# First batch's x turned as whole fp32 numbers, one head at a time, and split on the way out of PSUM

## The chip, the cores and the metric

The kernel runs on one core of one Trainium2 chip. The metric is the device time of one execution in microseconds (us). TensorE (PE) multiplies matrices, VectorE (DVE), ScalarE (ACT) and GpSimd (POOL) work elementwise, and SyncE (SP) issues every DMA of this kernel, in one order.

## The reference

For each of 8 batches and 8 heads, 512 tokens of x read 32 states, and the 32 states read the tokens:

```python
B, H, S, Ns, D = (8, 8, 512, 32, 64)
scores = scale * np.matmul(x, state.transpose(0, 1, 3, 2))      # then a softmax over the states
xread = np.matmul(a, state)
scores2 = scale * np.matmul(state, x.transpose(0, 1, 3, 2))     # then a softmax over the tokens
sread = np.matmul(a2, x)
return np.concatenate([xread, sread], axis=2)
```

The result, seen as 544 rows of 512 numbers for each batch, goes through a mixture of 4 single-head causal attention experts (head size 64, the two best experts of each row, weighted by a softmax of their gate logits):

```python
logits = x @ w_gate
topk = np.argpartition(-logits, K, axis=-1)[..., :K]            # K = 2
q = x @ wq[e]; k = x @ wk[e]; v = x @ wv[e]
scores = np.where(causal, -1000000000.0, scale * (q @ k.transpose(0, 2, 1)))
ye = a @ v @ wo[e]
out += mask[..., None] * w[:, :, kk:kk + 1] * ye
```

Inputs and output are fp32, the output has 8 x 544 x 512 numbers.

## The kernel before

**One list of steps.** The program first records every instruction as a step (class `Steps`), and `st.run(ORDER)` then issues them all from one line of a loop, which is why nearly every row of the profile names L265. `ORDER` holds three stored tables: the order of all steps, the engine that takes a step which two engines can do, and the buffer that each step gets. So the order on every engine, SP's DMAs among them, is the one that the tables say, and a changed table moves instructions anywhere in the program.

**Numbers in two parts.** A product in TensorE takes fp16 operands, so a fp32 number is kept as a high fp16 part (ACT writes it) and a low one (DVE's SCALAR_TENSOR_TENSOR, or two POOL instructions, subtract the high part), made by `hi_lo`. Three products of parts stand for one product.

**A batch.** `load(b)` fetches x in two halves of 256 tokens (tile `xn`, 512 KB each, two buffers) and the states (`sn`). `front(b)` makes the block matrix `bd` of the states, splits x into `xh` (`parts_of_x`), turns it into `xT`, multiplies `xT` with `bd` to the scores, makes their softmax (`eb`, then `at`), and from these and the split weights `wn` the keys `kt`, the values `v` and the queries `qf`, which are split into `qh` and turned by a DMA transpose into `qm`. Its last part, `side(b)`, does the same for the states (`state_scores`, `e2`, `a`, a DMA transpose into `a2t`, a product `a2t,xh`). `probs(b)` is the expert attention (scores `kt,qm`, probabilities `p`, split `ph`, DMA transpose `pt`), `reads(b)` multiplies `v,pt`, weighs the result (`z`, `zh`, DMA transpose) and multiplies with `wo`; every second batch `tail` treats the 2 x 32 state rows.

**The first batch** is made another way. Its `xh` is turned by TensorE, as 16-bit numbers (32 transposes `identh,xh`, 128 x 128 each), and copied out of PSUM into `xT` by ACT or DVE; `bd0` and `xT` give the scores of one 128-token tile and two heads at a time; the products `gs`, `at` behind the softmax are fp32. The weights are loaded behind both halves of the first x (`marks["l"]`):

```python
wfs, wg_ = load_weights(marks["l"])
```

Ahead of it TensorE gets matmuls on a tile of zeros (the `FILL` list: 35 of them, `bank<-zeros` in the profile), whose result nobody reads.

Of the kernel before, what the change touches and what calls it, by code (L numbers as in the profile page):

```python
# [18 lines left out]
CFG = dict(FILL=(1.0, 1.4, 1.8, 2.2, 2.6, 3.0, 3.4, 3.8, 4.2, 4.6, 5.0, 8.0, 8.5, 9.0, 9.5, 10.0, 10.5, 11.0, 11.5, 13.6, 14.0, 14.4, 14.8, 15.2, 15.6, 16.0, 16.4, 17.0, 17.4, 17.8, 18.2, 18.6, 19.0, 41.0, 41.2), RA=-1, RG=1, RV=2, RK=2, ZL=3, GP=1, PT=4, ZM=4, SM=4, QM=4, SIDE=32, FB=1, PX=1, PA=2, LB=1, xn=2, W0=-33, PACE=37.0, LAG=2,  # L19
# [9 lines left out]
        "!%AF+6QCvrLV4T*MQJ%agjKi!CPENxh1IwmgQ)`6!WCE%>tiw62F<V>Rl?fX3b#XJObQKf4YtPS*aR!%T1*BZR0o@48;ry)a2+<p;#8iVL0z"
        "nZ>#-%)!_riN8es`)i%;M=l%yBX2{&MSd<oy69lnAt7@0fcBZ$JK=rxp~H_!ne!&~T%PvJYfgR;~Ie?Uj<iCwV=Zp8P%*bn>SPl&*uVH5s>F"  # L30
        "Yp_N;AZ>^192!0!frSgKfoUl{0qY{B3C5E!Pp-SC*p8){0JkkDviW&Sc$e^6B>Y@U>t^GO&W!OlW;Un$1vQAV{j@W#^M?@4QC?Z3=H6Z5SyD"
        ")be@ORXck7oxI7;h;B1V_ad<q&;{cq1+i?yyqv{k7BTG~akF_W{Zo}rZ5ToH-+<}WQKE~k5*ny^CbgWJBIR-|c1h^RMPzp?lEoccw#$Ff`>r"
        "zT=NfB@-cBIbKiDF@8szO~T6?Ub1v<rLV8mdo`DI!LsM7SG!&{}Fht!NK+qjj_wThmG0hYcwTwW0kOlMmo}YD5PyF-E~tm>M@wV~UN3@H9rH"
# [235 lines left out]
def state_read_then_moe_attention(ctx: ExitStack, tc: tile.TileContext, x, state, w_gate, wq, wk, wv, wo, out):  # L269
# [220 lines left out]
    def load(b, after=None):  # L490
# [561 lines left out]
```

## Time and profile before

| | us |
|---|---|
| median of 3 runs | 307.17 |
| the three runs | 307.17, 305.06, 308.19 |
| the profiled execution | 310.0 |
| its span in the trace | 308.2 |

The profiled execution is a run of its own, 2.8 us above the median; 1.8 us of it lie outside the span. Busy times and stamps below are counted in us from the start of the span. The mean granted TensorE clock of the span is 0.983 of full speed (2.4 GHz; the lower of its two levels, 1.2 GHz, reads as 0.5).

### The profile page before, as it was taken

What the parts mean: (1) busy time and instruction counts of PE and PEld (TensorE: products, weight loads), DVE (VectorE), ACT (ScalarE), POOL (GpSimd) and SP (SyncE); (2) the same over time, 40 slices, a digit from 0 to 9 for tenths busy, and PEclk for the clock granted to TensorE, in tenths of its full rate; (3) what the DMA queues carried; (4) which work ended last, traced back from release to release, by engine and by line L of the source; (5) the groups of instructions that cost most, each with busy time, mean ns of one, the idle gap of its engine ahead of it and who ended that gap; (6) DMA issues with size and microseconds to landing.
All of it is one profiled execution on the core that took longest, in us unless ns stands there. A gap on an engine that the chain in (4) does not pass through costs nothing.

```text
span 308.2 us, 8993 instructions
## 1 busy us (share of the span) xinstructions
PE 285.8 (93%) x3323; PEld 193.7 (63%) x3323; DVE 260.0 (84%) x745; ACT 226.1 (73%) x690; POOL 151.9 (49%) x222
## 2 busy tenths in 40 slices
PE   8988799978999997999989799989999899999995
PEld 3555486655664756567764579747667668666763
DVE  3899799896899968799979979999997987878653
ACT  4678698886988967688977797879859955536532
POOL 7132454747663754549846874356366313511200
PEclk9999989997999997999999999999999999999999
DMA  8969689999799999889999999698368497398974
GB/s 194 223 124 203 154 156 183 234 177 172 138 202 203 168 180 213 171 177 197 207 142 245 185 234 175 125 185 178 83 146 176 91 209 126 95 172 205 184 213 152
DMA packets 165260, 53.95 MB, mean 175 GB/s; under 512 B 144096, under 2 KB 160736, under 8 KB 165216
## 3 DMA queue, kind: packets, MB, share of 16 engines
q1 hardware_dynamic: 165216, 53.37, 89.2%
q8 instruction: 26, 0.43, 0.6%
q14 instruction: 18, 0.15, 0.2%
HBM read 11.02 MB, written 8.91 MB: 65 GB/s over the span
## 4 chain that ended last, share of the span: by engine, by line
PE 46%; DVE 21%; DMA 14%; ACT 12%; issue 4%; POOL 3%; SPq 0%; DVEq 0%; ACTq 0%; POOLq 0%
PE bank L265 46%; DMA xn<-in_x_dram 4%; DMA qm<-qh 4%; DVE mx L265 3%; DMA a2t<-a 3%; ACT p L265 2%; ACT z L265 2%; DMA pt<-ph 2%; DVE xh L265 2%; DVE mb L265 2%; DMA z<-zh 1%; DVE eb L265 1%; DVE qf L265 1%; DVE sbm L265 1%; DVE z L265 1%
## 5 line engine op out<-in xcount | busy, mean ns | idle before, releaser
L265 PE MATMUL bank<-kt,qm 128*128 128x128 f16 (+7 forms) x384 | 48.4, 305 | 4.6 <-DMA qm<-qh 4.0
L265 PE MATMUL bank<-gs,at 128*128 128x260 f16 (+3 forms) x368 | 50.7, 284 | 1.1 <-DVE eb L265 0.7
L265 PE MATMUL bank<-wo_n,z 128*128 128x512 f16 (+1 forms) x198 | 46.5, 373 | 2.8 <-DMA z<-zh 2.3
L265 PE MATMUL bank<-v,pt 128*128 128x192 f16 x480 | 45.5, 251 | 2.7 <-DVE kt L265 1.5
L265 PEld LDWEIGHTS <-pt 128*128 128x128 f16 x480 | 41.0, 100 | 6.7 <-issue 4.0
L265 PEld LDWEIGHTS <-at 128*128 128x128 f16 x336 | 32.1, 98 | 8.5 <-issue 2.3
L265 ACT ACTIVATE p<-bank,mx 128x128 f32<-128x128 f32 (+3 forms) x64 | 33.3, 526 | 4.3 <-DVE mx L265 3.9
L265 PEld LDWEIGHTS <-qm 128*128 128x128 f16 (+1 forms) x384 | 23.5, 98 | 18.7 <-DMA qm<-qh 4.6
L265 DVE TENSOR_REDUCE mx<-bank 128x1 f32<-128x128 f32 (+3 forms) x64 | 28.8, 478 | 7.7 <-PE bank L265 7.3
L265 POOL TENSOR_TENSOR ph<-p,ph 128x768 f16<-128x768 f32 (+1 forms) x15 | 28.1, 1875 | 7.4 <-ACT ph L265 4.8
L265 PEld LDWEIGHTS <-z 128*128 128x128 f16 x198 | 18.1, 98 | 21.7 <-DMA z<-zh 3.8
L265 ACT ACTIVATE o<-bank 128x512 f32<-128x512 f32 x30 | 17.8, 596 | 11.9 <-PE bank L265 11.8
L265 ACT ACTIVATE z<-bank,c 128x64 f32<-128x64 f32 x87 | 20.4, 320 | 6.8 <-PE bank L265 6.1
L265 ACT ACTIVATE xh<-xn 128x512 f16<-128x512 f32 x32 | 19.1, 629 | 7.3 <-DMA xn<-in_x_dram 6.4
L265 PE MATMUL bank<-at,gs 128*128 128x512 f16 (+1 forms) x92 | 24.2, 399 | 0.3 <-DVE m L265 0.3
L265 DVE SCALAR_TENSOR_TENSOR xh<-xn,xh 128x512 f16<-128x512 f32 x27 | 19.5, 741 | 3.9 <-ACT xh L265 3.8
L265 POOL TENSOR_TENSOR qh<-qf,qh 128x768 f16<-128x768 f32 x11 | 18.4, 1680 | 5.0 <-ACT qh L265 4.9
L265 POOL TENSOR_TENSOR eb<-eb,sbm 128x512 f32<-128x512 f32 x11 | 12.4, 1130 | 13.4 <-DVE sbm L265 12.0
L265 POOL TENSOR_TENSOR z<-z 128x128 f32<-128x128 f32 x15 | 7.0, 468 | 21.7 <-DVE z L265 9.5
L265 ACT ACTIVATE ph<-p 128x768 f16<-128x768 f32 (+1 forms) x17 | 15.6, 918 | 2.1 <-DMA pt<-ph 2.1
L265 ACT ACTIVATE gs<-bank 128x512 f16<-128x512 f32 (+2 forms) x29 | 13.7, 496 | 4.7 <-PE bank L265 4.6
L265 PEld LDWEIGHTS <-xh 128*128 128x128 f16 x416 | 15.1, 101 | 2.1 <-issue 0.8
(213 smaller groups left out, 663.9 us busy)
## 6 DMA issues: line engine op xcount, KB each, us to landing
out_dram<-o SPq DMA_DIRECT2D x33, 256.0 KB, 2.8
xn<-in_x_dram SPq DMA_DIRECT2D x16, 512.0 KB, 4.8
sn<-in_state_dram SPq DMA_DIRECT2D x8, 64.0 KB, 4.2
p<-in_moe_wo_dram SPq DMA_DIRECT2D x2, 256.0 KB, 4.0
z<-zh SPq DMA_TRANSPOSE x29, 2.8
xT<-xh SPq DMA_TRANSPOSE x28, 3.3
p<-in_moe_wq_dram SPq DMA_DIRECT2D x1, 384.0 KB, 5.3
p<-in_moe_wv_dram SPq DMA_DIRECT2D x1, 384.0 KB, 4.8
```

The costliest lines, as they stand in the source:

```text
L265: f(**{k: v.ap() if isinstance(v, View) else v for k, v in kw.items()})
```

## The change

**The first batch's x.** TensorE now turns `xn` itself: 16 fp32 transposes of 128 x 128, each one head of 256 tokens (two tokens beside each other in a partition). Four of them fill a PSUM bank; ACT writes the high part out of it into `xT`, DVE the low part. `xT` is seen as [P, 2, 2, H, P] for it. The states of batch 0 are loaded twice beside each other (`sn2`, two DMAs of 64 KB), turned by two transposes, and written into `bd2`; the scores come as 24 products of 64 columns for each half of x. `xh` of batch 0 is still needed by the product `a2t,xh`, and its 4 pairs of splits now stand behind `marks["A"]`, which is behind the softmax. `state_scores` of batch 0 has 48 products of 256 columns in place of 24 of 512, with two maxima and two sums to be joined.

**Around it.** `xn` has four buffers in place of two; the weights are fetched in the order wv, wk, wq, and behind the first half of x alone; `tmt` has one buffer in place of two; 11 of the 35 zero matmuls have another due time; and all three tables of `ORDER` are new.

What it does to SP's queue at the start of the program (`xn` is x, `sn` the states, `p` the staged weights). Before:

```order
L265 DMA xn_88<-in_x_dram 128x8x128
L265 DMA xn_89<-in_x_dram 128x8x128
L265 DMA sn_87<-in_state_dram 128x2x64 x2
L265 DMA p_0_112<-in_moe_wq_dram 128x12x64
L265 DMA p_1_113<-in_moe_wk_dram 128x4x64
L265 DMA wg_111<-in_moe_w_gate_dram 128x4x4
L265 DMA p_2_114<-in_moe_wv_dram 128x4x64
L265 DMA p_2_114<-in_moe_wv_dram 128x12x64
L265 DMA p_1_113<-in_moe_wk_dram 128x12x64
L265 DMA p_0_112<-in_moe_wq_dram 128x4x64
L265 DMA xn_88<-in_x_dram 128x8x128
```

and now:

```order
L265 DMA xn_89<-in_x_dram 128x8x128
L265 DMA sn_0_88<-in_state_dram 128x2x64 x2
L265 DMA xn_90<-in_x_dram 128x8x128
L265 DMA xn_91<-in_x_dram 128x8x128
L265 DMA sn_87<-in_state_dram 128x2x64
L265 DMA p_0_115<-in_moe_wv_dram 128x12x64
L265 DMA wg_114<-in_moe_w_gate_dram 128x4x4
L265 DMA p_0_115<-in_moe_wv_dram 128x4x64
L265 DMA xn_92<-in_x_dram 128x8x128
L265 DMA p_1_116<-in_moe_wk_dram 128x12x64
L265 DMA p_2_117<-in_moe_wq_dram 128x4x64
L265 DMA p_2_117<-in_moe_wq_dram 128x12x64
```

The two state loads stand ahead of the second half of x, and both halves of batch 1's x (`xn_91`, `xn_92`) ahead of the weights wk and wq.

DVE's first work on data, before:

```order
L265 SCALAR_TENSOR_TENSOR xh_92<-xn_88,xh_92 128x512 x2
L265 SCALAR_TENSOR_TENSOR xh_93<-xn_89,xh_93 128x512 x2
L265 COPY xT_96<-bank_79 128x512
L265 SCALAR_TENSOR_TENSOR bd_0_90<-bank_82,bd_0_90 64x4x32 x2
L265 COPY xT_96<-bank_84 128x512 x2
L265 TENSOR_REDUCE mb_116<-bank_80 128x16
```

and now:

```order
L265 SCALAR_TENSOR_TENSOR xT_99<-bank_82,xT_99 128x512
L265 SCALAR_TENSOR_TENSOR xT_99<-bank_83,xT_99 128x512
L265 SCALAR_TENSOR_TENSOR bd_0_93<-bank_86,bd_0_93 64x256 x2
L265 SCALAR_TENSOR_TENSOR xT_99<-bank_80,xT_99 128x512
L265 SCALAR_TENSOR_TENSOR xT_99<-bank_81,xT_99 128x512
L265 TENSOR_REDUCE mb_119<-bank_84 128x16
```

Three copies are gone from the stretch ahead of the scores, and four low parts of `xh` stand behind the softmax now (three of them on DVE).

SP's queue where the queries of batch 1 are turned (`qm`), before:

```order
L265 DMA_TRANSPOSE pt_0_155<-ph_153 128x12x128
L265 DMA_TRANSPOSE pt_0_168<-ph_154 128x12x128
L265 DMA_TRANSPOSE xT_96<-xh_94 128x8x128
L265 DMA xn_89<-in_x_dram 128x8x128
L265 DMA_TRANSPOSE qm_134<-qh_142 128x12x128
```

and now:

```order
L265 DMA xn_90<-in_x_dram 128x8x128
L265 DMA xn_89<-in_x_dram 128x8x128
L265 DMA_TRANSPOSE pt_0_160<-ph_158 128x12x128
L265 DMA_TRANSPOSE pt_0_173<-ph_159 128x12x128
L265 DMA_TRANSPOSE xT_99<-xh_95 128x8x128 x2
L265 DMA_TRANSPOSE qm_137<-qh_145 128x12x128
```

The load of x that stood directly ahead of the first `qm` is ahead of both `pt` transposes now, and a second `xT` transpose stands in its place.

The diff, without the stored tables:

```diff
-CFG = dict(FILL=(1.0, 1.4, 1.8, 2.2, 2.6, 3.0, 3.4, 3.8, 4.2, 4.6, 5.0, 8.0, 8.5, 9.0, 9.5, 10.0, 10.5, 11.0, 11.5, 13.6, 14.0, 14.4, 14.8, 15.2, 15.6, 16.0, 16.4, 17.0, 17.4, 17.8, 18.2, 18.6, 19.0, 41.0, 41.2), RA=-1, RG=1, RV=2, RK=2, ZL=3, GP=1, PT=4, ZM=4, SM=4, QM=4, SIDE=32, FB=1, PX=1, PA=2, LB=1, xn=2, W0=-33, PACE=37.0, LAG=2,
+CFG = dict(FILL=(1.0, 1.4, 1.8, 2.2, 2.6, 3.0, 3.4, 3.8, 4.2, 4.6, 5.0, 8.0, 8.5, 9.0, 9.5, 10.0, 10.5, 11.0, 11.5, 13.6, 14.0, 14.4, 41.0, 41.2, 7.0, 7.0, 7.0, 7.0, 7.0, 7.0, 7.0, 7.0, 7.0, 7.0, 7.0), RA=-1, RG=1, RV=2, RK=2, ZL=3, GP=1, PT=4, ZM=4, SM=4, QM=4, SIDE=32, FB=1, PX=1, PA=2, LB=1, xn=4, W0=-33, PACE=37.0, LAG=2,
            FRONT=1.5, FSPAN=1.0, TSPAN=1.3, TOFF=1.2, KT=3, p32=3, ph=2, at=1, et=1, gs=1, xh=4, a2=1, o=4, sn=1, qf=2,
...
         st.dma(wg_, w_gate.rearrange("(k p) e -> p k e", p=P), 0.2, after=after)
-        for w in (wq, wk, wv):
+        for w in (wv, wk, wq):
...
             sns[b // 2] = st.buf("sn", [P, 2, 2, D], F32, bufs=CFG["sn"])
-            load_state(b, after)
+            if b == 0:
+                twice["sn"] = st.buf("sn2", [P, 2, 2, D])
+                for r in range(2):
+                    st.dma(twice["sn"][:, :, r], state[0].rearrange("(j c) n d -> n j c d", c=2), 0.4)
+            else:
+                load_state(b, after)
             if b > 0:
...
             xns[b].append(xn)
+            if u == 0:
+                marks["h"] = marks["l"]
         if b == 0:
...
-        bd = st.buf("bd0", [P, 2, H // 2, 2 * NS], F16) if whole else st.buf("bd", [P, 2, P], F16, bufs=2)
...
-        if whole:
-            fill(bd, 0.0)
-        tp = bank("tp")
-        st.transposes([(tp[:, :P], sn[:, b % 2].rearrange("p c d -> p (c d)"))], ident, 0.11, into=[bd])
...
-        turned = tp[:, :P].rearrange("p (n j) -> p j n", n=NS)
+        tp = bank("tp")
         if whole:
+            sn = twice["sn"]
+            bd = st.buf("bd2", [P, 2, 2, 2 * P], F16)
+            fill(bd, 0.0)
+            st.transposes([(tp[:, c * P:(c + 1) * P], sn[:, c].rearrange("p r d -> p (r d)")) for c in range(2)], ident, 0.22, into=[bd])
+            for r in range(2):
+                hi_lo(2 * P, bd[HC[r], 0, r], bd[HC[r], 1, r], tp[HC[r], :2 * P], 128.0)
+            bd32 = st.buf("bd32", [P, P], bufs=CFG["FB"])
             for c in range(2):
-                hi_lo(P, bd[HC[c], 0, :, c * NS:(c + 1) * NS], bd[HC[c], 1, :, c * NS:(c + 1) * NS], turned[HC[c]], 128.0)
+                act(P, by_head(bd32[HC[c]]), tp[HC[c], c * P:(c + 1) * P].rearrange("p (n j) -> p j n", n=NS), scale=128.0)
         else:
+            bd = st.buf("bd", [P, 2, P], F16, bufs=2)
+            st.transposes([(tp[:, :P], sn[:, b % 2].rearrange("p c d -> p (c d)"))], ident, 0.11, into=[bd])
+            turned = tp[:, :P].rearrange("p (n j) -> p j n", n=NS)
             hi_lo(P, by_head(bd[:, 0]), by_head(bd[:, 1]), turned, 128.0)
-        if whole:
-            bd32 = st.buf("bd32", [P, P], bufs=CFG["FB"])
-            act(P, by_head(bd32), turned, scale=128.0)
-        xh = [st.buf("xh", [P, 2, 2, DM], F16, bufs=CFG["xh"], use=u) for u in range(2)]
-        xT = st.buf("xT", [P, T, 2, H // 2, P], F16, bufs=1)
+        xh = [st.buf("xh", [P, 2, 2, DM], F16, bufs=CFG["xh"], use=u + 2 * whole) for u in range(2)]
+        xT = st.buf("xT", [P, T, 2, H // 2, P], F16, bufs=1, seen=([P, 2, 2, H, P], [
+            ("rearrange", ("p t a j q -> p (t a j) q",), {}), ("rearrange", ("p (u a h) q -> p u a h q",), dict(u=2, a=2))]) if whole else None)
...
-        for t in range(T):
-            parts_of_x(t)
-            if b < CFG["PX"]:
-                tp = bank("xt")
-                ts = tp.bitcast(F16).rearrange("p (a j q) -> p a j q", a=2, j=H // 2)
-                st.transposes([(ts[:, a, j, :], xh[t // 2][:, t % 2, a, j * P:(j + 1) * P]) for a in range(2) for j in range(H // 2)],
-                              identh, 0.43, into=[xT[:, t]])
-                marks["t"] = len(st.all) - 1
-                for a in range(2):
...
-            else:
...
+        if whole:
+            for u in range(2):
+                for k in range(2):
+                    tp = bank("xt")
+                    heads = range(4 * k, 4 * k + 4)
+                    st.transposes([(tp[:, h % 4 * P:(h % 4 + 1) * P], xn[u][:, h, :]) for h in heads], ident, 0.44, into=[xT[:, u, :, 4 * k:4 * k + 4]])
+                    marks["t"] = len(st.all) - 1
+                    hi_lo(DM, xT[:, u, 0, 4 * k:4 * k + 4], xT[:, u, 1, 4 * k:4 * k + 4], tp.rearrange("p (h q) -> p h q", q=P), 128.0)
+        else:
+            for t in range(T):
+                parts_of_x(t)
+                st.dma(xT[:, t].rearrange("p a j q -> p (a j) q"), xh[t // 2][:, t % 2].rearrange("p a c -> p (a c)"), 0.9, transpose=True)
         if b == 0:
...
             st.behind = None
-            wfs, wg_ = load_weights(marks["l"])
+            wfs, wg_ = load_weights(marks["h"])
             marks["w"] = len(st.all) - 1
...
             e2s[b] = new_e2()
-            sas = state_scores(of_head, xT, e2s[b], [eb])
...
+        elif whole:
+            scs = [bank(f"sc{u}") for u in range(2)]
+            for u in range(2):
+                st.mm([(scs[u].rearrange("p (r c j n) -> p c j r n", r=2, c=2, n=NS)[:, h % 2, h // 2], xT[:, u, a, h, :],
+                        bd[:, cc].rearrange("p r (c n j) -> p c j r n", c=2, n=NS)[:, h % 2, h // 2], n == 0, n == 2)
+                       for h in range(H) for n, (a, cc) in enumerate(PROD)], (24, 2 * NS, 128, 1), into=[eb])
         else:
...
                         for n, (a, cc) in enumerate(PROD):
-                            if whole:
-                                g.append((scs[u].rearrange("p (t c j n) -> p t j c n", t=2, c=2, j=H // 2)[:, t % 2, j], xT[:, t, a, j, :], bd[:, cc, j, :], n == 0, n == 2))
-                                continue
                             for c in range(2):
-                                g.append((scs[c][:, t * P + j * NS:t * P + (j + 1) * NS], xT[HC[c], t, a, j, :], of_head(c, cc, j), n == 0, n == 2))
-                st.mm(g, (24, 2 * NS, 128, 1) if whole else (48, NS, 64, 2), into=[eb])
+                                g.append((scs[c][:, t * P + j * NS:t * P + (j + 1) * NS], xT[HC[c], t, a, j, :], bd[HC[c], cc, HJ[j]], n == 0, n == 2))
+                st.mm(g, (48, NS, 64, 2), into=[eb])
         for u in range(2):
...
-                st.mm([(gp[HJ[j], :n], of_head(c, a, j), wn[HC[c], cc, j, lo_:hi_], i == 0, i == 2)
+                st.mm([(gp[HJ[j], :n], bd[HC[c], a, HJ[j]], wn[HC[c], cc, j, lo_:hi_], i == 0, i == 2)
...
             st.behind = marks["A"]
+            if whole:
+                for t in range(T):
+                    parts_of_x(t)
             if b == 0:
...
                 load_wo(marks["l"])
-        side(b, of_head, xT, xh)
+        side(b, bd, xT, xh, whole)
         st.behind = None
...
-    def state_scores(of_head, xT, e2s, into):
...
-        st.mm([(sa[HJ[j]], of_head(c, a, j), xT[HC[c], :, cc, j, :], i == 0, i == 2)
+        if whole:
+            mr = st.buf("mr", [P, 2, 2])
+            er = st.buf("er", [P, 2, 2])
+            st.mm([(sas[r][HJ[j], c * 256:(c + 1) * 256], bd[HC[r], a, r].rearrange("p (c n j) -> p c j n", c=2, n=NS)[:, c, j],
+                    xT[HC[r], :, cc, 2 * j + c, :], i == 0, i == 2)
+                   for c in range(2) for i, (a, cc) in enumerate(PROD) for j in range(H // 2) for r in range(2)], (48, 256, 64, 8), into=[e2] + into)
+            for r in range(2):
+                dve(512, nc.vector.tensor_reduce, out=mr[:, r], in_=sas[r].rearrange("p (c x) -> p c x", c=2), axis=AX.X, op=ALU.max, negate=True)
+            dve(2, nc.vector.tensor_tensor, out=m2, in0=mr[:, 0], in1=mr[:, 1], op=ALU.min)
+            small(2, m2, m2, 0.0, 2.0 ** -17)
+            for c in range(2):
+                for r in range(2):
+                    act(256, e2[:, c].rearrange("p (u r q) -> p r u q", u=2, r=2)[:, r], sas[r][:, c * 256:(c + 1) * 256].rearrange("p (u q) -> p u q", u=2),
+                        AF.Exp, bias=m2[:, c:c + 1], scale=2.0 ** -17, accum_out=er[:, r, c:c + 1])
+            dve(2, nc.vector.tensor_tensor, out=s2, in0=er[:, 0], in1=er[:, 1], op=ALU.add)
+            return
+        st.mm([(sa[HJ[j]], bd[HC[c], a, HJ[j]], xT[HC[c], :, cc, j, :], i == 0, i == 2)
                for i, (a, cc) in enumerate(PROD) for j in range(H // 2) for c, sa in enumerate(sas)], (24, 512, 64, 8), into=[e2] + into)
...
-    def side(b, of_head, xT, xh):
+    def side(b, bd, xT, xh, whole):
...
             e2s[b] = new_e2()
-            state_scores(of_head, xT, e2s[b], [])
...
         dve(4, nc.vector.tensor_scalar, out=m4, in0=wg, scalar1=0.0, scalar2=None, op0=ALU.is_gt)
-        mt = st.buf("tmt", [P, 2, P], BF16, bufs=2)
+        mt = st.buf("tmt", [P, 2, P], BF16, bufs=1)
```

## Rows read from the trace of the kernel before

**Rows 1.** The page, part 1: busy us, share of the span and instructions.

```profile
PE 285.8 (93%) x3323; PEld 193.7 (63%) x3323; DVE 260.0 (84%) x745; ACT 226.1 (73%) x690; POOL 151.9 (49%) x222
```

**Rows 2.** Windows: length, busy PE, PEld, DVE, ACT, POOL, granted clock, DMA share, GB/s.

```profile
20.00:25.00 5.00, 5.00 (x28) 3.27 (x28) 5.00 (x12) 5.00 (x14) 2.80 (x5) 1.00 0.84 111
...
30.00:35.00 5.00, 4.13 (x38) 2.53 (x37) 2.83 (x8) 1.94 (x4) 0.70 (x3) 1.00 0.59 165
35.00:40.00 5.00, 3.71 (x38) 2.98 (x38) 5.00 (x14) 4.88 (x16) 4.33 (x6) 0.72 0.65 160
40.00:50.00 10.00, 10.00 (x147) 7.46 (x145) 9.49 (x22) 8.77 (x27) 4.99 (x5) 0.97 0.92 164
...
60.00:80.00 20.00, 16.13 (x207) 11.20 (x204) 16.81 (x37) 16.13 (x49) 12.49 (x14) 0.91 1.00 174
```

**Rows 3.** Timeline to 20 us: start, us, engine, work, count, [idle before <-releaser].

```profile
1.18 5.99 PE L265 MATMUL bank<-zeros 128*128 128x512 bf16 x15 [1.18 <-DVE zeros L301]
...
1.87 1.96 SPq L265 DMA_DIRECT2D sn<-in_state_dram  x2
...
4.91 1.15 ACT L265 ACTIVATE xh<-xn 128x512 f16<-128x512 f32 x2 [2.90 <-DMA xn<-in_x_dram]
...
6.77 1.15 ACT L265 ACTIVATE xh<-xn 128x512 f16<-128x512 f32 x2 [0.72 <-DMA xn<-in_x_dram]
...
7.01 1.06 PE L265 MATMUL bank<-identh,xh 128*128 128x128 f16 x16
...
10.22 1.66 PE L265 MATMUL bank<-bd,xT 128*128 128x64 f16 x47 [0.47 <-DVE bd L265]
...
16.43 0.69 DVE L265 TENSOR_TENSOR eb<-eb,sbm 128x512 f32<-128x512 f32 x1
...
17.61 1.04 PE L265 MATMUL bank<-ident,eb 128*128 128x128 f32 x8
```

**Rows 4.** Timeline, 27 to 46 us.

```profile
32.91 0.72 ACT L265 ACTIVATE a<-e,s 128x512 f16<-128x512 f32 x1 [2.73 <-DMA a2t<-a]
...
35.01 1.01 DVE L265 TENSOR_TENSOR qf<-bank,m 128x384 f32<-128x384 f32 x2
...
36.29 0.38 PE L265 MATMUL bank<-kt,less 128*128 128x512 f16 x1 [2.16 <-ACT kt L265]
...
38.71 5.12 SPq L265 DMA_TRANSPOSE qm<-qh  x2
...
44.12 1.21 PE L265 MATMUL bank<-kt,qm 128*128 128x128 f16 x12
```

**Rows 5.** Timeline, 60 to 72 us.

```profile
60.90 2.75 DVE L265 SCALAR_TENSOR_TENSOR xh<-xn,xh 128x512 f16<-128x512 f32 x2
...
61.46 1.64 POOL L265 TENSOR_TENSOR qh<-qf,qh 128x768 f16<-128x768 f32 x1 [0.52 <-ACT qh L265]
...
63.68 0.37 SPq L265 DMA_DIRECT2D xn<-in_x_dram  x1
64.10 2.76 SPq L265 DMA_TRANSPOSE qm<-qh  x1
...
70.86 1.72 PE L265 MATMUL bank<-kt,qm 128*128 128x128 f16 x12 [2.59 <-DMA qm<-qh]
```

**Rows 6.** Tile qm, then tile xn: from a DMA's issue to its landing.

```profile
DMA to landing us min/median/max: 3.6/4.1/6.7
...
DMA to landing us min/median/max: 4.2/4.8/6.5
```

**Rows 7.** Timeline around the other waits of PE, 114 to 156 us.

```profile
114.57 0.63 ACT L265 ACTIVATE xh<-xn 128x512 f16<-128x512 f32 x1 [2.78 <-DMA xn<-in_x_dram]
...
116.40 0.82 PE L265 MATMUL bank<-gs,at 128*128 128x260 f16 x6 [0.74 <-DVE eb L265]
...
118.76 3.72 PE L265 MATMUL bank<-v,pt 128*128 128x192 f16 x24 [1.53 <-DVE kt L265]
...
155.36 1.15 PE L265 MATMUL bank<-kt,qm 128*128 128x384 f16 x6 [1.41 <-DMA qm<-qh]
```

More of the change, by code (lines that the diff above doesn't have):

```diff
@@ L29 @@
[L29 to L33, printed above, removed]
@@ new lines @@
+        "h<azQ4@0O=twREOM94KhL@$OomM0fayv2!>)<7>YoCr~oyf5j2DnPzge?5JrK<P#B{^W@rsvpa~Sk($Ex&Lo}!YT_HLYfRfM#Vn8#9300vR#"
+        "Da3r9AZOTC<rZ}G`53^Pz+i^2`mHUp*^&M%1{(KKw0Pry&woX!AU5C#i&1Qfg*Ssj=?Fo0$ZUoY=RTe9gf35*ag9O4feuS7y^f3AM}9Y*c0}"
+        "{85jxM;5uxE0dNC)Ls`5DC2<zqhCOfuhQb{Pg;ID6cEdcF4R>J-+=KgY7RJLlcmPLXEL?;G@DK*U5*Q5IVH7-q9WVjP;USm^!{8vyhdwX|#z"
+        "6>`$DJ@2qVgm-52GQ7CPM`r4pX2nEQ4U`2UFn!T!Lv(3*$f#EP%(b8Y<!lm<~^%60U_Xm;p~=Ce+47uozb1WmpPpU^z6w)wlxU!a9ftbud0u"
+        "#+8r&)?h+d59=@yB!=Qt7uRAEcm`E)6>NZoupaAS3EF@qsXkW404PO)Pz{qpYupGeumLv3>evQ1Vq2_%$)Gf~#P-+_H(@($g=J_nHp80O0UK"
@@ L446, in load_weights @@
         st.dma(wg_, w_gate.rearrange("(k p) e -> p k e", p=P), 0.2, after=after)
-        for w in (wq, wk, wv):
+        for w in (wv, wk, wq):
             wf = stage()
-            wfs.append(wf)
+            wfs.insert(0, wf)
             for e, to, n in (1, 0, E - 1), (0, E - 1, 1):
@@ L479, in state_read_then_moe_attention @@
     xns, sns, marks = {}, {}, {}
-    consts = {}
+    consts, twice = {}, {}
     def bank(use):
@@ L540, in parts_of_x @@
                   xn[t // 2][:, :, t % 2 * D:(t % 2 + 1) * D], 128.0, psum=False)
-        for t in range(T):
-            parts_of_x(t)
-            if b < CFG["PX"]:
-                tp = bank("xt")
-                ts = tp.bitcast(F16).rearrange("p (a j q) -> p a j q", a=2, j=H // 2)
-                st.transposes([(ts[:, a, j, :], xh[t // 2][:, t % 2, a, j * P:(j + 1) * P]) for a in range(2) for j in range(H // 2)],
-                              identh, 0.43, into=[xT[:, t]])
-                marks["t"] = len(st.all) - 1
-                for a in range(2):
-                    kw = dict(out=xT[:, t, a], in_=ts[:, a])
-                    st.either([("ACT", 0.478, (nc.scalar.activation, dict(func=AF.Copy, scale=1.0, **kw))), ("DVE", 0.6, (nc.vector.tensor_copy, kw))])
-            else:
-                marks["x", b] = st.dma(xT[:, t].rearrange("p a j q -> p (a j) q"), xh[t // 2][:, t % 2].rearrange("p a c -> p (a c)"), 0.9, transpose=True)
+        if whole:
[10 more added lines that the diff above has]
+                st.dma(xT[:, t].rearrange("p a j q -> p (a j) q"), xh[t // 2][:, t % 2].rearrange("p a c -> p (a c)"), 0.9, transpose=True)
         if b == 0:
@@ L714, in new_e2, with state_scores @@
         return (st.buf("e2", [P, 2, S], F32, bufs=CFG["n_e2"]), st.buf("m2", [P, 2], F32, bufs=2), st.buf("s2", [P, 2], F32, bufs=2))
-    def state_scores(of_head, xT, e2s, into):
+    def state_scores(bd, xT, e2s, into, whole=False):
         e2, m2, s2 = e2s
         sas = [bank(f"sa{c}") for c in range(2)]
-        st.mm([(sa[HJ[j]], of_head(c, a, j), xT[HC[c], :, cc, j, :], i == 0, i == 2)
+        if whole:
[15 more added lines that the diff above has]
+        st.mm([(sa[HJ[j]], bd[HC[c], a, HJ[j]], xT[HC[c], :, cc, j, :], i == 0, i == 2)
                for i, (a, cc) in enumerate(PROD) for j in range(H // 2) for c, sa in enumerate(sas)], (24, 512, 64, 8), into=[e2] + into)
@@ L727, in state_scores @@
         return sas
-    def side(b, of_head, xT, xh):
+    def side(b, bd, xT, xh, whole):
         if b not in e2s:
             e2s[b] = new_e2()
-            state_scores(of_head, xT, e2s[b], [])
+            state_scores(bd, xT, e2s[b], [], whole)
         e2, m2, s2 = e2s.pop(b)
```

83 lines of the change are left out of this document (41 added, 42 removed).

## The prediction

> **What bounds the kernel now.** I read the page's busy times first: TensorE works 285.8 us of a span of 308.2 [rows 1], and 22 us are left in which it doesn't, so a change outside TensorE can win only from those 22 us and from time at the lower clock. Then I read the windows, to see where PE is idle or slow. There are two such places in the first third: from 30 to 50 us the granted clock falls to 0.72 and 0.97, and from 60 to 80 PE is busy for 16.13 of 20 us at 0.91 [rows 2]. From 20 to 25 DVE and ACT are busy for all 5 us: what the prologue saves before 20 must pass these two engines [rows 2]. The timeline then tells who is waited for. In the prologue it is x: the first half lands at 4.91, the second at 6.77, and DVE and ACT carry it from there to the end of the scores, 11.88 (10.22 + 1.66), and of the softmax, 17.12 (16.43 + 0.69) [rows 3]. At 36.29 PE comes out of 2.16 us of idle time behind the first keys, and at 70.86 out of 2.59 behind the DMA that turns batch 1's queries [rows 4, 5]. Two later waits are at 116.40 and 118.76, and one of 1.41 at 155.36 [rows 7].
>
> Everything below is summed against the profiled execution, 310.0 us: 308.2 of span and 1.8 around it. It is 2.8 above the median of the runs; the last step takes that off.
>
> **A: the prologue.** *Transposes.* 32 fp16 ones go, the first 16 of which take 1.06 us, 66 ns each; 16 fp32 ones come, and such ones take 130 ns each today (1.04 for 8) [rows 3]. 2.1 us against 2.1: nothing. *Splits.* Four ACT passes and four DVE passes over 512 columns stand where four of each stood, now out of PSUM; I price them by the SBUF rows at 0.58 (1.15 for 2) and 0.69 [rows 3]. The eight copies into xT (three on DVE) go, but xh of batch 0 comes back behind the softmax as four ACT passes of 0.58 and three low parts on DVE, 2.1 us, and one on POOL. DVE so carries as much as before up to the first queries, and the later part of it lies where DVE is full. *Loads.* The two state loads take 1.96 of SP's time [rows 3] and are now ahead of x's second half. Its issue moves from about 1.3 to 3.2, and with 4.2 to a landing at the fastest [rows 6] it lands at 7.4; if it is as much later as it is issued, at 8.7. Behind it come 0.5 of transposes, ACT's 0.58, two passes of 0.69 and half of the scores, 0.83: 3.3 us, so the scores end at 10.7 to 12.0, where they ended at 11.88; the first half's splits hide under the wait for the second. I take 11.3, a gain of 0.6, and for the bounds -1.2 and +1.0 (a landing at 9.7, by the slowest of 6.5 [rows 6]). *The zeros.* 15 of them stood ahead of the first transposes, at 0.40 each, and 11 stand there now: 4.4 us, to 5.6, later than the first half's landing; the transposes would start then, 1.4 earlier than at 7.01 [rows 3], and wait for the second half anyway. Nothing.
>
> *Passed on.* The first queries (35.01) stand behind full DVE and ACT and behind the side chain's transpose, for which ACT sits idle 2.73 us [rows 4]. If the 0.6 passes through, PE's idle time of 2.16 shrinks to about 1.6. What follows it is the lower clock: 28% of 5 us and 3% of 10, or 1.7 us lost [rows 2]. After a wait of 1.41 products of 384 columns took 0.19 each (1.15 for 6), after one of 1.53 products of 192 columns took 0.155 each (3.72 for 24) and not half of 0.19 [rows 7]; so 1.6 lies where it can go either way; I take a third of the 1.7. A in all: -1.2; bounds -2.9 (1.2 and 1.7) and +1.7 (the 1.0, and one more pass of 0.7 for the two extra exponentials and joins of the state softmax). A larger gain is shut off: the first kt,qm cannot run before its DMA, issued at 38.71, has landed, 3.6 us later at the fastest [rows 4, 6], and that chain is older than the prologue's 0.6.
>
> **B: the wait at 70.86.** Before, the queries' split ends on POOL at 63.10 (61.46 + 1.64), but SP holds a load of x that waits until 63.65 for its buffer, which DVE's two xh passes free (60.90 + 2.75, twice their usual length, beside POOL's pass). The queries' transpose goes out at 64.10, next to a load of 512 KB, and lands 6.7 us later, at 70.81; the median is 4.1 [rows 5, 6]. With four buffers the load stands five rows earlier, and the transpose goes behind two xT transposes, which wait for the same DVE passes. If they hold nothing up it is issued at 63.2 and lands at 67.3, before PE is ready (68.27, which is 70.86 - 2.59): the 2.59 are gone, and the lower clock behind them, 9% of 20 us or 1.8 [rows 2], 4.4 in all. If it is issued a whole such issue (2.76 [rows 5]) behind 63.65, it lands at 70.5, and 2.2 of idle time and the clock stay: 0.4. The first xT needs only the first of the two passes, so I lean to the near end: -3.5, bounds 0 and -4.4.
>
> **C: the waits at 116.40 and 118.76.** ACT has sat 2.78 us for batch 5's x until 114.57, and PE loses 0.74 and 1.53 behind that [rows 7]. In the new order this load is still directly behind the tail's transpose `tpt` on SP, which waits for the attention of batches 0 and 1. I take 0; bounds 0 and -4.1 (the two waits, and a clock loss like B's 1.8).
>
> **D: the rest of the new tables.** PE's order behind the prologue only swaps neighbours, DVE and ACT lose 16 and 12 instructions and POOL gets 21. I take 0, and 2 us to either side: a POOL pass beside DVE's doubles that one, as the 2.75 shows [rows 5], and each of these can land on a wait.
>
> **The sum:** 310.0 - 1.2 - 3.5 = 305.3 for an execution like the profiled one, 302.5 for the median. Part of the 2.8 between them may be these same stalls, since a landing of 6.7 is the longest of its tile; I give back 1.0: **303.5 us**.
>
> **Rivals.** *1, the wait only changes its neighbour.* The two xT transposes hold SP until the DVE passes are through, B gives 0.4, A the 0.6 of the scores: 306.2. For it speaks that both xT and the old load wait for the same 60.90 + 2.75. Against it, that the 512 KB load is gone from beside the transpose.
>
> *2, C goes too*, since x of batch 5 finds a free buffer and A and B shift the tail: 3.5 of the 4.1, 300.0. Against it stands SP's order.
>
> *3, the transposes don't keep the clock up.* TensorE's first real work is then fp32 transposes, with four zeros fewer ahead. In the trace of before, the fp16 transposes ran at 66 ns each [rows 3], and the granted clock was still 1.00 from 20 to 25 [rows 2]. If it fell to the lower level, the transposes (2.1), the scores (1.66) and the turning of eb (1.04) would take twice as long: +4.8, 308.3. The Trainium skill, "TensorE: Matmul & The Clock Gate", Part 4: PE-mode transpose, says that the full clock does not engage for transposes since they don't count as busy; it speaks for this rival, and the 66 ns with the granted clock at 1.00 do not, so by that rule alone it gets a small chance.
>
> *4, slower: the last weights come late.* wk and wq are now behind 1.05 MB of batch 1's x; at the 164 GB/s of 40 to 50 us [rows 2] that is 6.4 us. DVE's idle time in 30 to 35 (2.17 of 5) is the slack of the first queries, and 4.2 us of slip would be left. Then A's 1.2 is lost, PE waits 4.2 longer, and a wait so long brings the lower clock back, 1.8: 303.5 + 7.2 = 310.7. It decides from a slip of 3.7 us on; then the time passes that of before. Against it: the weights' first issue is no longer behind both halves of x, and batch 1's x is what the next steps need first.
>
> **How the numbers follow.** Forecast 0.42, with a range of its own of 301.5 to 305; rival 1 0.30; rival 2 0.08; rival 3 0.07; rival 4 0.13. One per cent, 3.1 us, is about what a measurement of this kernel can tell from no change: faster is below 304.1, slower above 310.2. Faster: rival 2 and nine tenths of the forecast, 0.46. Slower: rival 4, most of it, and a little of D's ends, 0.13. Same: the rest, 0.41. The range goes from 298.0 (rival 2 with D's 2 us) to 309.5, which leaves out rival 4 and few others.
>
> **What would show it.** In the profile after, the second half of x lands at 7.4 to 8.7 and the scores end near 11.3; the last multiplication of eb ends at 16.5; the first queries come at about 34.4, and the windows from 35 to 50 show a granted clock above 0.9 if A's clock part is right. PE's wait at batch 1's first kt,qm is under 1 us and 60 to 80 stands at 1.00 if B is right; a wait of over 2 us there, behind two xT, is rival 1. ACT still waits 2 to 3 us for x near 110 to 115 if C is right. PE idle for more than 2 us ahead of the key and query products between 20 and 35 is rival 4, a granted clock of 0.5 between 7 and 20 rival 3. I am wrong if a stall arises that the trace of before doesn't have: of D I know only the order.

## The result and the profile after

The changed kernel takes 304.41 us (median of 10 runs, 303.57 to 306.97), the kernel before 308.29 beside it (10 runs, 305.06 to 309.79): a ratio of 0.9902, 95% interval 0.9873 to 0.9931. That is 3.0 us by the ratio, which is taken over all runs, and 3.9 by the medians. The time is within the range and 0.9 us from the forecast. The profiled execution after is 304.6 us with a span of 302.6. The one shown of before (310.0) was more than 1.5% above the fastest run of its kernel, so part of its waits belong to that execution alone; a second trace of the same kernel (307.75, span 306.0) stands beside it below and is the one compared with.

The windows after, columns as in [rows 2]:

```profile
10.00:15.00 5.00, 5.00 (x77) 3.39 (x75) 3.87 (x7) 2.25 (x7) 3.95 (x15) 0.73 1.27 233
...
35.00:40.00 5.00, 4.47 (x67) 1.77 (x66) 5.00 (x10) 4.43 (x17) 4.30 (x7) 1.00 1.02 136
40.00:50.00 10.00, 9.72 (x144) 6.89 (x140) 9.34 (x24) 8.65 (x26) 6.57 (x7) 1.00 0.99 162
...
60.00:80.00 20.00, 16.70 (x234) 12.75 (x232) 18.24 (x46) 17.32 (x51) 14.53 (x17) 1.00 1.10 178
```

The lower clock of [rows 2] is gone from 35 to 50 and from 60 to 80; a new one stands from 10 to 15 (0.73; it ends in the next window, 0.93). PE's timeline after:

```profile
1.18 4.63 PE L265 MATMUL bank<-zeros 128*128 128x512 bf16 x11 [1.18 <-DVE zeros L301]
5.65 1.04 PE L265 MATMUL bank<-ident,xn 128*128 128x128 f32 x8
...
7.74 1.09 PE L265 MATMUL bank<-ident,xn 128*128 128x128 f32 x8 [0.19 <-DMA xn<-in_x_dram]
...
9.37 2.98 PE L265 MATMUL bank<-bd,xT 128*128 128x64 f16 x47 [0.48 <-DVE bd L265]
...
44.81 1.16 PE L265 MATMUL bank<-kt,qm 128*128 128x128 f16 x12 [0.28 <-DMA qm<-qh]
...
66.69 0.19 PE L265 MATMUL bank<-xt_tail,wn 128*128 128x64 f16 x1 [0.87 <-ACT xt_tail L265]
68.14 1.53 PE L265 MATMUL bank<-xt_tail,wn 128*128 128x64 f16 x47 [1.26 <-DVE xt_tail L265]
69.50 1.15 PE L265 MATMUL bank<-kt,qm 128*128 128x128 f16 x12
...
101.14 2.81 PE L265 MATMUL bank<-gs,at 128*128 128x256 f16 x24 [1.35 <-DVE v L265]
```

The rows with f32 are products of whole fp32 numbers: that numbers are split in two fp16 parts is the kernel's choice, and TensorE takes fp32 operands too. Against [rows 3]: the transposes cost what was forecast, and x's second half lands at 7.7; but the scores take 2.98 us where they took 1.66. Against [rows 5]: the 2.59 us behind batch 1's `qm` are gone; 2.1 us of waits for `xt_tail` stand just ahead of it, and the product starts at 69.50, 0.8 later than in the second trace of before (68.67, below). Of [rows 7] the 1.53 at 118.76 is gone, and a wait of 1.35 has come at 101. SP around batch 1's queries, after:

```profile
60.85 2.92 SPq L265 DMA_TRANSPOSE xT<-xh  x2
64.11 4.52 SPq L265 DMA_TRANSPOSE qm<-qh  x2
```

`qm` goes out at 64.11, at the time of [rows 5] (64.10) and 2.1 later than in the second trace of before:

```profile
61.53 0.37 SPq L265 DMA_DIRECT2D xn<-in_x_dram  x1
61.96 2.87 SPq L265 DMA_TRANSPOSE qm<-qh  x1
```

It goes out behind the POOL pass of `qh`, which now ends at 64.09. What it no longer has is a load beside it: it lands after 4.3 us, where both traces of before have 6.7.

DVE after, low parts of `xh` and first queries (the two at 17.92 and one of 24.07 are batch 1's):

```profile
17.31 0.69 DVE L265 TENSOR_TENSOR eb<-eb,sbm 128x512 f32<-128x512 f32 x1
17.92 1.28 DVE L265 SCALAR_TENSOR_TENSOR xh<-xn,xh 128x512 f16<-128x512 f32 x2
...
20.20 1.17 DVE L265 SCALAR_TENSOR_TENSOR xh<-xn,xh 128x512 f16<-128x512 f32 x1
...
24.07 1.28 DVE L265 SCALAR_TENSOR_TENSOR xh<-xn,xh 128x512 f16<-128x512 f32 x2
...
28.47 1.17 DVE L265 SCALAR_TENSOR_TENSOR xh<-xn,xh 128x512 f16<-128x512 f32 x1
...
30.71 0.68 DVE L265 SCALAR_TENSOR_TENSOR xh<-xn,xh 128x512 f16<-128x512 f32 x1
...
35.66 1.01 DVE L265 TENSOR_TENSOR qf<-bank,m 128x384 f32<-128x384 f32 x2
```

All four low parts of batch 0 are on DVE (the section on the change and the prediction said three), two of them at 1.17; in their stead one of batch 1's is on POOL, ahead of the softmax (11.08).

### The profile page after: what moved, and what is told of

Its sections match the earlier page's. It is cut to its first block, busy times and chain, and to the rows that moved or that the text cites. A ratio compares the mean times of both kernels' runs of the same rounds, so it can differ in the third digit from the quotient of the medians.

```text
span 302.6 us, 9013 instructions
## 1 busy us (share of the span) xinstructions
PE 285.0 (94%) x3332; PEld 191.7 (63%) x3332; DVE 256.4 (85%) x729; ACT 224.5 (74%) x680; POOL 167.1 (55%) x243
## 3 DMA queue, kind: packets, MB, share of 16 engines
HBM read 11.08 MB, written 8.91 MB: 66 GB/s over the span
## 4 chain that ended last, share of the span: by engine, by line
PE 40%; DVE 8%; POOL 4%; DMA 3%; ACT 2%; issue 2%; POOLq 0%; DVEq 0%; ACTq 0%
PE bank L265 40%; DMA qm<-qh 3%; DVE mx L265 1%; POOL qh L265 1%; DVE xh L265 1%; DVE gt L265 1%; POOL xh L265 1%; POOL ph L265 1%; POOL eb L265 0%; DVE qf L265 0%; DVE sbm L265 0%; ACT p L265 0%; DVE cmp L265 0%; DVE v L265 0%; DVE a L265 0%
## 5 line engine op out<-in xcount | busy, mean ns | idle before, releaser
L265 PE MATMUL bank<-v,pt 128*128 128x192 f16 x480 | 43.9, 246 | 1.6 <-ACT p L265 1.6
L265 PEld LDWEIGHTS <-pt 128*128 128x128 f16 x480 | 39.7, 98 | 5.3 <-issue 2.8
L265 POOL TENSOR_TENSOR ph<-p,ph 128x768 f16<-128x768 f32 (+1 forms) x13 | 24.6, 1889 | 7.3 <-ACT lg L265 3.8
L265 POOL TENSOR_TENSOR qh<-qf,qh 128x768 f16<-128x768 f32 x14 | 23.2, 1661 | 5.7 <-ACT qh L265 5.3
L265 POOL TENSOR_TENSOR zh<-z,zh 128x256 f16<-128x256 f32 x22 | 15.9, 722 | 18.6 <-ACT zh L265 15.4
L265 POOL TENSOR_TENSOR z<-z 128x128 f32<-128x128 f32 x22 | 11.4, 519 | 24.9 <-DVE z L265 10.7
L265 ACT ACTIVATE o<-bank 128x512 f32<-128x512 f32 (+1 forms) x31 | 18.1, 585 | 5.8 <-PE bank L265 5.6
L265 DVE TENSOR_TENSOR z<-bank,c 128x192 f32<-128x192 f32 x41 | 13.6, 345 | 7.3 <-PE bank L265 2.8
L265 ACT ACTIVATE z<-bank,c 128x64 f32<-128x64 f32 x69 | 16.3, 316 | 2.9 <-PE bank L265 1.6
L265 ACT ACTIVATE gs<-bank 128x512 f16<-128x512 f32 (+3 forms) x33 | 15.5, 489 | 2.8 <-PE bank L265 2.7
```

What stands on the lines that cost most here:

```text
L265: f(**{k: v.ap() if isinstance(v, View) else v for k, v in kw.items()})
```

## The experiments

Three theories: *Queue*, the gain is the load of x that leaves the place ahead of batch 1's query transpose; *Prologue*, it is the new turning of the first batch's x; *Order*, it is the rest of the new tables. The edits are made behind the decoding of the tables, by step number. Each ratio is to runs of the kernel before in the same session, over 6 to 12 runs of each kernel listed.

| run | us | ratio to before, 95% |
|---|---|---|
| e1_before_4_buffers | 306.74 | 0.9984 (0.9946 to 1.0022) |
| e2_before_load_earlier | 305.73 | 0.9925 (0.9894 to 0.9956) |
| e3_after_load_late | 305.33 | 0.9934 (0.9901 to 0.9967) |
| e4a_zeros_ahead | 306.70 | 0.9971 (0.9939 to 1.0003) |
| e4b_zeros_between | 306.54 | 0.9968 (0.9930 to 1.0007) |
| e5_weights_first | 310.58 | 1.0135 (1.0078 to 1.0192) |
| e6_bd2_in_rows | 304.56 | 0.9878 (0.9842 to 0.9914) |
| e7_old_start_new_rest | 303.44 | 0.9850 (0.9814 to 0.9885) |
| e8_low_parts_on_pool | 305.39 | 0.9919 (0.9888 to 0.9951) |
| e9_new_start_old_rest | 308.03 | 0.9993 (0.9956 to 1.0029) |
| e10_old_start_longer | 305.02 | 0.9898 (0.9866 to 0.9930) |

### The kernel before once more

No edit. 

> The kernel before, unchanged, for a second trace of it. The trace shown of before is of an execution of 310.0 us, 1.7 above the median of 308.3. If the wait of 2.59 us behind batch 1's query transpose and the lower clock behind it belong to every execution, this trace has them too, at about the same place. If they are what makes an execution slow, a trace nearer 306 lacks them, and then they can't be what the change removes.

One execution, 307.75 us. DVE, then PE, in the second trace of before:

```profile
16.50 0.69 DVE L265 TENSOR_TENSOR eb<-eb,sbm 128x512 f32<-128x512 f32 x1
...
32.51 1.01 DVE L265 TENSOR_TENSOR qf<-bank,m 128x384 f32<-128x384 f32 x2
```

```profile
34.40 0.38 PE L265 MATMUL bank<-kt,less 128*128 128x512 f16 x1 [0.89 <-ACT kt L265]
...
41.91 1.28 PE L265 MATMUL bank<-kt,qm 128*128 128x128 f16 x12
...
68.67 1.96 PE L265 MATMUL bank<-kt,qm 128*128 128x128 f16 x12 [2.54 <-DMA qm<-qh]
```

The wait for `qm` (2.54) is there again, with 0.91 from 60 to 80; it belongs to the kernel. The 2.16 at 36.29 is 0.89 here, the clock from 30 to 50 is 1.00, and the first `kt,qm` comes at 41.91 and not 44.12: that part of [rows 4] belonged to one execution, and so did the lower clock of [rows 2] from 35 to 50.

### The load ahead of batch 1's query transpose

e1, `xn=4` and the slots of `xn` in turn over four buffers:

```diff
+            b.slot = self.tags[b.tag][b.turn[1] % 4 if b.tag == "xn" else slot]
```

> The kernel before with four buffers for x, every step in its old place: the load of x directly ahead of batch 1's first query transpose no longer waits for a buffer, but is still on its way beside it. Theory Queue (the gain is the wait of SP ahead of that transpose): the transpose is issued about 0.9 us earlier, the wait at 70.86 falls from 2.6 to 1.7 or less; 306 to 307.5. If the load beside it makes the landing long, it still takes over 5.5 us. Rivals, Prologue (the gain is the new turning of the first batch's x) and Order (it is the other new places of the tables): nothing moves, 308.3.

e2, e1 and one step (1037, the load) moved ahead of the first `pt` (243):

```diff
+        steps.remove(1037)
+        steps.insert(steps.index(243), 1037)
```

> As the run with four buffers, and that one load of x stands five places earlier in SP's queue, where the changed kernel has it. The rest is the kernel before, first batch and all. Theory Queue: the wait behind batch 1's query transpose is gone and the granted clock from 60 to 80 us is 1.00; the whole 3.5 to 4.4 us, 304 to 305. Prologue and Order: 308.3, or the wait is gone here and comes back later.

e3, in the changed kernel, the same load (1042) back ahead of `qm` (419):

```diff
+        steps.remove(1042)
+        steps.insert(steps.index(419), 1042)
```

> The changed kernel with this one load put back directly ahead of batch 1's first query transpose; it has a free buffer there, so it doesn't wait, but is on its way beside the transpose. Theory Queue: the transpose takes 5.5 us or more to land and PE waits for it again, 305.5 to 307. If only the wait for the buffer mattered, and under Prologue and Order: 304.4.

PE in e1, e2 and e3, one fence each:

```profile
67.45 1.17 PE L265 MATMUL bank<-kt,qm 128*128 128x128 f16 x12 [1.19 <-DMA qm<-qh]
```

```profile
67.61 1.16 PE L268 MATMUL bank<-kt,qm 128*128 128x128 f16 x12 [0.61 <-DMA qm<-qh]
```

```profile
69.85 2.10 PE L268 MATMUL bank<-kt,qm 128*128 128x128 f16 x12
```

The buffers alone halve the wait (2.54 to 1.19): `qm` goes out at 61.12, 0.8 earlier, and with the load beside it still lands after 6.3 us. Their gain in time can't be told from none. With the load moved as well the wait is 0.61 and the ratio 0.9925, 2.3 us (I expected 3.5 to 4.4): *Queue* is shown, in a kernel whose first batch is the old one. By the means of their 12 runs, 307.1 and 305.4, e2 is 1.7 us ahead of e1. The traces can't rank these two, since e1's is of an execution of 304.88 us and e2's of one of 306.55.

In e3 the transpose lands after 5.7 us, as I expected, but PE doesn't wait for it, since it comes later to it (behind the `xt_tail` waits). The loss against the changed kernel, 0.3% or 0.9 us, lies within the intervals; I expected 305.5 to 307. So in the changed kernel the place of this load is not shown to be worth anything.

### The first scores and the clock

e4a and e4b, zeros issued again ahead of the first transposes (step 48), or between the groups (11) and ahead of the scores (95):

```diff
+        steps[steps.index(48):steps.index(48)] = [11] * 4
```

```diff
+        steps[steps.index(11):steps.index(11)] = [11] * 3
+        steps[steps.index(95):steps.index(95)] = [12] * 2
```

> The changed kernel with 15 matmuls on zeros ahead of the first transposes, as the kernel before has, in place of 11 (four are issued twice). In the trace after, the first scores take 2.98 us for 47 products where the trace before has 1.66, so TensorE ran them at its lower level. If the four zeros are what keeps the clock up, the scores take about 1.7 again, although the first transposes start 1.7 us later. If a gain in the prologue passes to the end, the whole is 1 us shorter, 303.4; if it is taken up by DVE and ACT, which are full behind it, 304.4. If transposes of fp32 don't keep the clock whatever stands ahead of them, the scores still take 2.9.

> The changed kernel with three more zeros between the two groups of transposes and two between the second group and the scores, where PE waits. If the fall of the clock comes from the stretch of transposes and short waits, the scores are back at about 1.7 us and end at 11.3 in place of 12.35. The first kt,qm, at 44.81 in the trace after, comes up to 1 us earlier if that passes through: 303.4. If not: 304.4.

The window and the scores in e4a:

```profile
10.00:15.00 5.00, 4.95 (x82) 3.80 (x81) 3.94 (x7) 2.55 (x8) 3.87 (x14) 1.00 1.19 228
```

```profile
9.60 2.98 PE L267 MATMUL bank<-bd,xT 128*128 128x64 f16 x47 [0.56 <-DVE bd L267]
```

At a granted clock of 1.00 the scores take 2.98 all the same, in e4b too; and in the trace after the clock is 1.00 from 9.37 to 12.2 and falls only as they end. So my reading of the trace after, that the clock made them slow, was wrong. Neither run is faster than the changed kernel; by their ratios both are about 0.7% slower. One thing that differs from before is the scores' moving operand (the one that is not loaded as weights), `bd2`, whose numbers lie 8 bytes apart. e6 writes them side by side; of its edit, which does the same to the reading in `state_scores`:

```diff
-                hi_lo(2 * P, bd[HC[r], 0, r], bd[HC[r], 1, r], tp[HC[r], :2 * P], 128.0)
+                part = [[v[:, c * P:(c + 1) * P].rearrange(q, n=NS) for v, q in ((bd[HC[r], 0, r], "p (j n) -> p j n"), (bd[HC[r], 1, r], "p (j n) -> p j n"),
+                         (tp[HC[r], :2 * P], "p (n j) -> p j n"))] for c in range(2)]
...
-                        bd[:, cc].rearrange("p r (c n j) -> p c j r n", c=2, n=NS)[:, h % 2, h // 2], n == 0, n == 2)
+                        bd[:, cc].rearrange("p r (c j n) -> p c j r n", c=2, n=NS)[:, h % 2, h // 2], n == 0, n == 2)
```

> The changed kernel with the states' block matrix of batch 0 written so that the 32 states of a head lie beside each other; the scores read them one beside the other and not every fourth number (8 bytes apart). Written by four ACT and four DVE passes of 128 columns in place of two of 256. With more zeros the first scores still took 2.98 us at a granted clock of 1.00, so theory Stride says that the way the operand lies costs 28 ns for each of 48 products: the scores take 1.7 us, first qf up to 1 us earlier, 303.5 to 304.4. If it isn't the stride (the order of the output, or weights from another layout of xT), they take 2.98 again.

```profile
9.21 2.21 PE L265 MATMUL bank<-bd,xT 128*128 128x64 f16 x48
```

The whole takes 2.21 and not the 1.7 that *Stride* gave, but the products are as fast as it said. Each has a weight load of its own (PEld), and the loads show their pace. First the trace of before, then after, then e6:

```profile
10.33 1.43 PEld L265 LDWEIGHTS <-xT 128*128 128x128 f16 x46 [0.68 <-ACT xT L265]
```

```profile
9.37 2.80 PEld L265 LDWEIGHTS <-xT 128*128 128x128 f16 x46 [0.60 <-issue]
```

```profile
9.11 1.02 PEld L265 LDWEIGHTS <-xT 128*128 128x128 f16 x26
10.35 0.41 PEld L265 LDWEIGHTS <-xT 128*128 128x128 f16 x12 [0.22 <-DVE xT L265]
10.95 0.35 PEld L265 LDWEIGHTS <-xT 128*128 128x128 f16 x10 [0.19 <-DVE xT L265]
```

A load takes 0.10 to 0.12 us itself, so one followed the other every 60 ns after (2.80 for 46) and every 28 to 30 ns in e6 (0.41 for 12, 0.35 for 10) and before (1.43 for 46). *Stride* is right: the way this operand lies makes up the whole difference. What is left of e6's 2.21 is 0.4 of waits for DVE's low parts of `xT`, which the faster products now run into. The first `qf` is at 35.09 and the first `kt,qm` at 44.26, both 0.6 earlier; the time stays within the interval of the changed kernel.

### The weights behind x

e5 moves both halves of batch 1's x (steps 316, 317) behind the last weight (92). 

> The changed kernel with both halves of batch 1's x behind all weights in SP's queue, as before. If the weights come late in the changed kernel (rival 4 of the prediction), the queries come earlier now: first qf before 35.66, 303 to 304. If batch 1's x is what the next steps need, its xT comes later by up to 4 us and the time goes to 305 to 306. If neither: 304.4.

ACT in e5:

```profile
17.57 0.63 ACT L272 ACTIVATE xh<-xn 128x512 f16<-128x512 f32 x1 [7.22 <-DMA xn<-in_x_dram]
```

7.2 us of ACT idle, with batch 0's `bd` and softmax queued behind this step, and PE waits 4.40 for `bd`; the first `kt,qm` comes at 52.42 (this trace is of 314.2 us, the median is 310.6) and the time is 1.35% above before. The new order needs batch 1's x early, since ACT splits it ahead of batch 0's softmax. That stall hides what earlier weights would win here; against rival 4 stands the trace after itself, where PE has no wait of over 0.7 us from 20 to 35.

### Start and rest apart

e7 and e10 keep the old order for 298 and 386 steps and take the new order, engines and buffers for the rest; e9 is the mirror. Nothing else is edited; the buffers were given out anew where two would have met.

> The kernel before with its first batch and its start as they are up to its first kt,qm (298 of 1959 steps in its own order, engines and buffers), and from there on the order, engines and buffers of the changed kernel; four x buffers. Theory Start-costs (the new first batch makes the first kt,qm 2.9 us later, 44.8 against 41.9 in the second trace of before, and the new order behind it wins about 6): first kt,qm at 42, and 301 to 302.5. Theory Prologue (the new first batch is what wins): 306 to 308. If the start's delay is hidden behind something that comes at a fixed time: 304.4.

> The mirror of the run with the old start: the changed kernel up to its first kt,qm (new first batch, its own order, engines and buffers), and from there on the order, engines and buffers of the kernel before, the load of x directly ahead of batch 1's first query transpose among them. Theory Start-costs: the first kt,qm comes at about 44.8 and the rest wins nothing, so the time is 1 to 3 us above that of the kernel before, ratio 1.003 to 1.01. Theory Prologue (the new first batch wins): ratio 0.985 to 0.993. If the start's delay is taken up in the next 25 us by waits that come anyway: ratio 0.998 to 1.003.

> As the old start with the new rest, but the old order goes on to the first transpose of pt (386 steps in place of 298), since in the run with 298 PE waits 1.50 us right behind the seam (for at on DVE) and 1.26 for xt_tail at 67, where the clock falls. If the seam is what gives back the 2.9 us that the old start is ahead, batch 1's first kt,qm comes before 68 and the time goes to 301.5 to 302.5. If that stretch is set by DVE's own work of batch 1, it comes at 69 again, and the time stays at 303.4.

PE in e7, in e9 and in e10:

```profile
43.66 1.09 PE L265 MATMUL bank<-kt,qm 128*128 128x128 f16 x11 [1.50 <-DVE at L265]
...
66.92 2.66 PE L265 MATMUL bank<-xt_tail,wn 128*128 128x64 f16 x47 [1.26 <-DVE xt_tail L265]
69.39 1.57 PE L265 MATMUL bank<-kt,qm 128*128 128x128 f16 x12
```

```profile
44.99 1.16 PE L265 MATMUL bank<-kt,qm 128*128 128x128 f16 x12 [0.73 <-DMA qm<-qh]
...
70.17 1.16 PE L265 MATMUL bank<-kt,qm 128*128 128x128 f16 x12 [1.78 <-DMA qm<-qh]
```

```profile
66.31 1.57 PE L265 MATMUL bank<-xt_tail,wn 128*128 128x64 f16 x48 [1.48 <-DVE z L265]
67.74 1.17 PE L265 MATMUL bank<-kt,qm 128*128 128x128 f16 x12
```

*Prologue* falls: the new start with the old rest is 0.9993. The new rest with the old start is 0.985 and 0.990, as fast as the whole change or faster; e7 has the lowest median of all, 303.44 (I expected 301 to 302.5), but its interval overlaps that of the changed kernel, and e10, meant to be better, isn't. *Start-costs* is half right: the start is 2.9 us late at the first `kt,qm`, and much of that is gone by 70 us (e9 is 1.5 behind the second trace of before there, e7 0.1 ahead of the changed kernel).

What takes it up isn't shown. DVE's work of batch 1 doesn't hold that stretch at 69: in e10 batch 1's first `kt,qm` comes at 67.74, as I expected if the seam was to blame, and still the time is 305.02 and not 301.5 to 302.5. In the traces e10's lead of 1.7 us over e7 is gone by batch 4, whose first `kt,qm` comes at 179.79 in e10 and 179.01 in e7.

### The low parts on POOL

e8 sets the engine of steps 180, 182, 184 and 186:

```diff
+        for n in (180, 182, 184, 186):
+            ways[n] = 1
```

> The changed kernel with the four low parts of batch 0's xh on GpSimd (two instructions each) in place of DVE, where they stand in the stretch before the first queries. If these 2.7 us on DVE are what delays the first qf (35.66 in the trace after, 32.51 in the second trace of before), it comes 1 to 2.5 us earlier and the time goes to 302.5 to 303.5, less what POOL beside DVE costs. If DVE is not what it waits for there: 304.4; if POOL's passes lengthen DVE's by more than they take off: 305.

DVE in e8:

```profile
19.39 2.47 DVE L268 SCALAR_TENSOR_TENSOR wn<-p,wn 128x256 f16<-128x256 f32 x3
...
36.65 1.01 DVE L268 TENSOR_TENSOR qf<-bank,m 128x384 f32<-128x384 f32 x2
```

The queries come 1.0 later, not earlier: beside POOL's passes DVE's own take much longer (three `wn` in 2.47, 0.82 each, where two take 0.95 in the trace after). The time shows no gain. It doesn't tell what the passes cost on DVE.

## Why the prediction was right, by its steps

**A (forecast -1.2, bounds -2.9 and +1.7) had the wrong sign where it was read.** Against the second trace of before the scores end 0.4 later (12.35 against 11.96), the softmax 0.8 (18.00 against 17.19), the first `qf` 3.1 and the first `kt,qm` 2.9. Two sentences failed. "DVE so carries as much as before up to the first queries": the copies that go had stood where DVE waited for x, and the four low parts came to where it is full; they take 3.7 us there (all `xh` passes 5.6 in place of 2.7), and from the softmax to `qf` DVE needs 17.7 us and not 15.3. That these passes are the whole of it is argued from the trace; e8 couldn't show it. And the scores were priced at 1.66 when their operand had another layout, +1.3; e6 shows that cause. The 0.6 for the clock came from the one execution profiled. At the end little of the 2.9 is left: e9 against before gives nothing, e7 against the changed kernel 0.5%, with intervals that overlap.

**B (-3.5) was right about the wait and the load beside the transpose, and too large.** e2 gives the four buffers and the load's place -2.3 us (0.9925) in the old kernel; in the changed one, putting the load back costs 0.9 (e3), not clear of noise. The wait for `qm` is gone, as said; but `qm` is not issued at 63.2 as the sum has it, because its POOL pass is later (62.25 in the trace after, 59.32 in the second trace of before), and its faster landing counts. With a load of x directly ahead of it that took 5.4 to 6.7 us (both traces of before, e1, e3, e9), without one 3.9 to 4.7 in eight traces and 5.5 in e2. The 1.8 for the clock doesn't hang on this wait: from 60 to 80 the granted clock is 1.00 in e1 and e9, with waits for `qm` of 1.19 and 1.78, and 0.91 in e3, e4a and e7, where PE doesn't wait for it; all three have waits for `xt_tail` just ahead, and so has the trace after at 1.00.

**C (0) was wrong in place, though not in size that can be told.** ACT's wait for x, 2.78 in [rows 7] and 1.84 in the second trace of before (at 112.36), is gone, and so are the two waits of PE. The trace after has others in their stead (1.35 at 101, 1.60 at 167).

**D (0 and 2 either way)** held the rest. The whole is -3.0 and the start 0 to +1.5; so the other places of the new order win 0.7 to 2.2 us if B is the -2.3 of e2, and more if it is less in the changed kernel, as e3 has it. In the traces the lead over the second trace of before grows by 1.8 us from batch 2's first `kt,qm` to batch 3's, and by 1.8 between those of batches 4 and 5. Which moves do it isn't settled, and so the cause of a good part of the gain is open.

**The rivals.** Rival 1 didn't happen: both `xT` transposes are through SP at 63.77, before POOL's pass ends, and the new waits two steps ahead, 0.87 and 1.26 for `xt_tail`, are behind ACT and DVE. Rival 2's sign came, C's waits are gone, but not its time, 300.0, since other waits came. Rival 3: the clock did fall to 0.50 from 12.5 to 15.5 in the trace after; with the same transposes it is 1.00 from 7 to 20 in e3, e8 and e9, and in e4a, e4b and e6; the rule of the Trainium skill ("TensorE: Matmul & The Clock Gate", Part 4: PE-mode transpose) is neither shown nor excluded by that, and the cost that looked like it was the layout. Rival 4's sign, PE idle for over 2 us between 20 and 35, is not in the trace after. (Its slip of 3.7 us leads to 310.2, the bound that the prediction calls slower, and not to the time of before.)

So the number was near in part by luck: A's loss mostly vanished, B's excess and D's gain cancelled, and 2.8, less 1.0 given back, was allowed for the profiled execution.

## What to carry to other kernels

A change that carries a new algorithm and a new order should be split along the order: here four buffers and one load moved five places in SP's queue win 2.3 us in the old kernel, where the whole change wins 3.0, and the new first batch, the part that the change is named for, wins nothing that can be measured. It should be split from both sides, too: put back in the changed kernel, the same load costs 0.9 us, within the noise. Work that leaves a stretch where an engine waits and returns where it is full isn't a wash, even if its sum is. And before a stall is priced, a second trace of the same kernel tells whether it is the kernel's or one execution's.

## What was not expected of the hardware

Matmuls of 64 columns whose moving operand has its fp16 numbers 8 bytes apart followed each other every 60 ns at a granted clock of 1.00; with the numbers side by side, every 28 to 30 ns, as in the kernel before. The mean of a group hid that: 63 and 46 ns, since the faster group has waits inside.
